# An adaLN block with linear attention and a GEGLU FFN: small stretches of the middle stage joined, loads around the second LayerNorm put in another order, and one bfloat16 run for each pair of the down projection

## The chip, the core and the metric

The kernel runs on one NeuronCore of a Trainium2 chip. A core has a matrix engine (TensorE, in profiles PE, with its weight loads as PEld), a vector engine (VectorE, DVE), a scalar engine (ScalarE, ACT), GpSimd (POOL) and SyncE (SP), which here issues nearly all DMAs. The engines run side by side and meet at semaphores. The metric is the device time of one execution in microseconds (us); lower is better.

## The reference

S = 2048 rows, D = 1024, 32 heads of 32, F = 3584; all inputs are bfloat16.

```python
def _A_ref(x, wqkv, wo):                       # linear attention
    qkv = (x @ wqkv).reshape(B, S, 3, H, Dh).transpose(2, 0, 3, 1, 4)
    q, k, v = qkv
    phi = lambda t: jnp.where(t > 0, t + 1, jnp.exp(t)) + 1e-06
    pq, pk = phi(q), phi(k)
    kv = jnp.einsum('bhsd,bhse->bhde', pk, v)
    z = jnp.einsum('bhsd->bhd', pk)
    num = jnp.einsum('bhqd,bhde->bhqe', pq, kv)
    den = jnp.einsum('bhqd,bhd->bhq', pq, z)[..., None] + 1e-06
    return (num / den).transpose(0, 2, 1, 3).reshape(B, S, D) @ wo

def _B_ref(x, w_gate, w_up, w_down):           # GEGLU FFN
    return _gelu(x @ w_gate) * (x @ w_up) @ w_down

mod = (_silu(c) @ w_mod).reshape(1, 6, 1, -1)
sa, ca, ga, sb, cb, gb = (mod[:, i] for i in range(6))
h = _layernorm(x) * (1 + ca) + sa
x = x + ga * _A_ref(h, A_wqkv, A_wo)
h = _layernorm(x) * (1 + cb) + sb
x = x + gb * _B_ref(h, B_w_gate, B_w_up, B_w_down)
```

## The kernel before

Every operation is recorded first, as an `Op` with its engine, the bytes it reads and writes, and what it must wait for (`Sched.op`). Each engine then runs its own list in order; `Sched.reorder` moves DVE, ACT and POOL operations between the first K tiles and the start of LN2 by planned costs, and everything behind it runs in the order in which it was recorded. SP runs its DMAs in order too, and a DMA takes one of eight lanes in turn and waits for the one that used the lane before (`Sched.dma`), so at most eight are under way.

Rows are tiled in 16 chunks of 128 and 4 groups (sg) of 4 chunks. The stages, with TensorE's time in the profiled execution:

- K and Q, to 127 us: LN1, modulation, K and Q products, phi. Values that depend on `c` are summed on DVE meanwhile.
- M, 127 to 191: instead of V, M = pk^T x is formed in 24 tiles of 16 matmuls (`m_tile`, L895, banks 0 to 3 of PSUM in turn), transposed by DMA (`m_t`, mtb) and multiplied with Wv (`kv_prod`, L913). Between tiles stand small stretches, set out by tile number in `HOOK` (L1302): rows of the modulation (`mod_rows`, L840, 32 columns of the array at a time), the denominators (`den`, L1240), and kv folded into Wo (`w2_pair`, L1201). `mod_pass` (modp) makes sb and cb, `gb_rows` (gbr) makes gb; `mod_pass` stores its row to HBM and loads it back by partition (sbT, cbT). `den` stores 1/den to HBM, and `rb_load` (L1260) brings it back, broadcast over partitions, in four DMAs of 256 KB for each half group; RB has two buffers, for even and odd groups.
- Wo, 191 to 241: `pq_scale` (L1273, DVE, four operations for a half group) multiplies pq by 1/den; `wo_mm` (L1283) multiplies chunk by chunk with the folded Wo into banks 2(c%4) and the next; x1 (L1291, DVE) adds the residual and gives the row sums. LN2 of the first 8 chunks runs beside it, one step each: mean on POOL, Square on ACT (`ln2_stats`, L674), xhat on ACT into one of four buffers xl (`ln2_rows`, L660), a DMA transpose (T2) into h2a or h2b, modulation on DVE (`mod2`, L724) or ACT. The Square writes the same buffer xl of its chunk, so that of chunk c+4 waits for T2 of chunk c. `SLOT` lists what stands behind each chunk.
- FFN, 241 to 600: `unit` (L1458) is one 256-wide strip of gate and up for half of the rows, by a Strassen-Winograd scheme of seven products of half size: P1 and P2 in bfloat16, the others of sums (`s_sum` of rows, L1413; `t_sum` of weights, L1433) in fp32r. Chunks 14 and 15 of Wo stand inside unit 0.
- Down, 600 to 777: the same scheme for pairs of chunks (`d_pair`, L1672 through `d_prod`, 14 matmuls a product, pairs 0 to 7): sums of y on DVE (`d_s`, L1648; sum k feeds P5, P6, P7, P3, P4 for k = 0 to 4, two buffers SB in turn), sums of weights (`d_t`, L1621), partial results added in PSUM (`d_add`, L1695), results scaled by gb and added to x (`evac`, L1576 and L1577). `y_in` loads y (ya0, ya1), `x_in` loads x (xq0 to xq3). In one pair the order is P1, P5, P6, P2, P7, P3, P4: P1 and P2 are bfloat16, so there are two bfloat16 runs.

Of the kernel before, what the change touches and what calls it, by code (L numbers as in the profile page):

```python
# [15 lines left out]
CPG = NCH // NSG  # L16
# [314 lines left out]
def bass_adaLN_cond__linear_attn_block__geglu_ffn__prompt_kernel(  # L331
# [18 lines left out]
    with ExitStack() as es:  # L350
# [554 lines left out]
        def m_t(g):  # L905
            i = g % 2
            tdma(Q, MTB[i][:, :, :], MB[g][:, :], r_mb(g), r_mtb(i), f"mT{g}")

        def kv_prod(g, bank):
            i = g % 2  # L910
            o = None
            for dc in range(NDC):
                o = sch.op(T, lambda e, dc=dc: e.matmul(PS(bank, 0, P), WV[:, g, dc, :], MTB[i][:, dc, :],  # L913
                                                        start=(dc == 0), stop=(dc == NDC - 1)),
                           rd=r_wv(g) + r_mtb(i), pwr=(pr(bank) if dc == 0 else ()), note=f"kv g{g} dc{dc}")
            pset_writer(bank, o)
            z = 64 * (g % 2)
            for h in range(2):
                a, gz = 64 * h, g // 2 * 2 + h
                sch.op(V, lambda e, a=a, gz=gz: e.tensor_tensor(KVT[z:z + 64, gz, 0:64], ps_all[a:a + 64, bank * 512 + a:bank * 512 + a + 64], BMASK[a:a + 64, a:a + 64], ALU.mult),  # L920
                       prd=pr(bank), rd=r_sm("bmask"), wr=r_kvt(gz, gz + 1), note=f"kvt{g}", overwrite_ok=True)
# [270 lines left out]
        def z32():  # L1192
            sch.op(V, lambda e: e.tensor_tensor(Z32[:], BM32[:], ZCOLS[:, :].unsqueeze(2).to_broadcast([P, NG, NH]), ALU.mult),
                   rd=r_sm("bm32") + r_sm("zcols"), wr=r_sm("z32"), note="z32")

        def w2_pair(i, b0=4):
            for hf in range(2):
# [6 lines left out]
            for r in range(2):  # L1204
                b, g = b0 + 2 * r, 2 * i + r
                w_, p_ = W2[:, g, :], ps_all[:, b * 512:(b + 2) * 512]
                eng = V if i > 1 and r else A
                sch.op(eng, lambda e, w_=w_, p_=p_, eng=eng: e.activation(w_, p_, ACTF.Copy) if eng == A else e.tensor_copy(w_, p_),
                       prd=pr(b) + pr(b + 1), wr=r_w(OFF_WK, "w2", g), note=f"w2cp{g}")
# [15 lines left out]
        def mod_pass():  # L1225
            assert mdone[0] >= 48 and not late
            mod_rows(((2, 4, 5, hl_src),))
            o_r = mod_store(4, 5, MROW[1], r_2k(OFF_ROW + 2048, "mrow1"), 1)
            for dst, nt, a0 in ((SBT, "sbT", 0), (CBT, "cbT", 2)):
                sch.dma(Q, lambda e, dst=dst, a0=a0: e.dma_start(dst[:, :], scr_row[1, a0:a0 + 2, :].rearrange("a (b p) -> p (a b)", p=P)),  # L1230
                        wr=r_sm(nt), deps=[o_r], note=nt)

# [33 lines left out]
        GH = [((0, 2), (2, 4)), ((4, 6), (6, 8))]  # L1266

        def pq_scale(sg, h, gs):
            i, t0 = sg % 2, h * HW
            for g0, g1 in gs:  # L1270
                ap = PQ[sg][:, g0:g1, t0:t0 + HW]
                rng = r_pq(sg, g0, g1, t0, t0 + HW)
                sch.op(V, lambda e, ap=ap, i=i, h=h, g0=g0, g1=g1: e.tensor_tensor(ap, ap, RB[i][:, h, g0:g1, :], ALU.mult),  # L1273
                       rd=rng + r_rb(i, h, g0, g1), wr=rng, deps=rb_ops[sg, h], note=f"pqs{sg}.{h}.{g0}")

        x1_ops, s_ops = {}, {}

        def wo_mm(c_, b0, gs):
# [9 lines left out]
            if gs[-1] == NG - 1:  # L1288
                for half in range(2):
# [11 lines left out]
        tiles = [(g, k) for g in range(4) for k in range(3)] + [(g, 0) for g in range(4, NG)] + [(g, k) for g in range(4, NG) for k in (1, 2)]  # L1301
        HOOK = {0: "ga", 6: "kv0", 10: "kv1", 11: "w0", 13: "kv2", 15: "modp kv3 z32", 16: "den0", 17: "w1 rb0.0 rb0.1", 18: "",  # L1302
                19: "kv4", 20: "den1 ps0.0", 21: "gbr", 22: "ps0.1", 23: "rb2.0"}
        st = {}

        def hook_run(f):
            if f[:2] == "kv":
                kv_prod(int(f[2:]), 4)
            elif f == "ga":
                ga_pass()  # L1310
            elif f == "gbr":
                assert mdone[0] == 64
                gb_rows()
            elif f == "modp":
                mod_pass()
            elif f == "z32":
                z32()
            elif f[:3] == "den":
                st[int(f[3:])] = den(int(f[3:]), 5)
                st[int(f[3:])]()  # L1320
            elif f[:2] == "ps":
                pq_scale(int(f[2]), int(f[4]), GH[0] + GH[1])
            elif f[:2] == "rb":
                rb_load(int(f[2]), (int(f[4]),))
            elif f[0] == "w":
                w2_pair(int(f[1:]))

        for n, (g, k) in enumerate(tiles):
# [19 lines left out]
            for f in HOOK.get(n, "").split():  # L1348
                hook_run(f)
        wo_mm(0, 0, [0, 1, 2, 3])  # L1350
        w2_pair(2)
# [16 lines left out]
        def wt_dma(u):  # L1368
            i, f0 = u % 2, u % NFP * 256
            for t, v_ in enumerate((wg_v, wu_v)):  # L1370
                sch.dma(Q, lambda e, t=t, v_=v_: e.dma_start(WT[i][:, t, :, :], v_[:, :, f0:f0 + 256]), wr=r_wt(i, t, t + 1), note=f"wt{t} u{u}")

# [224 lines left out]

        pq_scale(2, 0, GH[0] + GH[1])

# [55 lines left out]
        def d_prod(ca, b0, k, own=None, js=None):  # L1655
            b = b0 + {1: 0, 2: 0, 5: 3, 6: 2, 7: 2, 4: 2, 3: 1}[k] if own is None else own
            i = {1: None, 2: None, 5: 0, 6: 1, 7: 2, 3: 3, 4: 4}[k]
            o = None
            js = range(nj(ca)) if js is None else js
            for j in js:  # L1660
# [5 lines left out]
                else:  # L1666
# [3 lines left out]
                    if i == 4:  # L1670
                        dst = dst.rearrange("p (h c) -> p h c", h=2)
                o = sch.op(T, lambda e, l_=l_, r_=r_, j=j, dst=dst: e.matmul(dst, l_[:, 0, :], r_, start=(k in (1, 5) or own is not None) and j == js[0], stop=j == js[-1], skip_group_check=True),  # L1672
                           rd=rl + rr, pwr=(pr(b) if j == js[0] else ()), note=f"down P{k} c{ca} j{j}", overwrite_ok=True)
# [30 lines left out]
        def d_pair0(hook):  # L1704
            parts = parts_of(0)
            for k in (2, 6, 5, 0, 7, 3, 13, 11, 12, 4):
# [13 lines left out]
                hook(k)  # L1720

        def d_pair(i, hook):
            ca, b0 = 2 * i, i % 2 * 4
# [6 lines left out]

            for k in (1, 5, 6, 2, 7, 3, 4):
                if last and k == 3:
                    d_prod(ca, b0, 3, None, range(6, NDJ))
                    evac_part(*parts[1])
                    continue
                d_prod(ca, b0, k)
                if k == 1:
                    d_cp(b0 + 2, b0, "dpcp")
                elif k == 5:
                    d_ecp(b0 + 3)  # L1740
                    d_s(ca, 2)
                elif k == 6:
                    d_add(b0 + 1, b0 + 2)
                    d_s(ca, 3)
                    y_next(0)
                elif k == 2:
                    evac(*parts[0])
                elif k == 7:
                    d_add(b0 + 3, b0 + 2)
                    d_s(ca, 4)  # L1750
                    y_next(1)
                    evac(*parts[3])
                elif k == 3:
# [130 lines left out]
        def hooks(i):  # L1884
            def hook(k):
                more = i + 1 < 2 * CPG
                if i == 1:
                    if k == 1:
                        d_t(2, 5)
                        d_t(2, 6)  # L1890
                    if k in (6, 2, 7):
                        d_t(4, {6: 4, 2: 5, 7: 6}[k])
                    if k in (6, 7):
                        n = 1 if k == 6 else 2
                        evac(*parts_of(0)[n])
# [12 lines left out]
        for i in range(1, 2 * CPG):
            d_pair(i, hooks(i))
# [75 lines left out]
```

## Time and profile before

| what | value |
|---|---|
| runs | 783.5, 783.53 and 1619.89 us; median 783.53 |
| the profiled execution, first to last instruction (span) | 780.9 us; its own time is not listed beside it |
| granted TensorE clock | 1.000 |
| TensorE in the first 24 us | warm-up matmuls, transposes and waits for the first loads |
| HBM read and written | 92.55 and 23.35 MB, 148 GB/s over the span |

Busy time of engines in five stretches around the start of LN2 (us of busy time; DMA is the mean busy share of the 16 DMA engines):

| stretch | length | PE | DVE | ACT | DMA share | GB/s |
|---|---|---|---|---|---|---|
| 190 to 206 | 16 | 15.79 | 10.98 | 4.86 | 0.92 | 198 |
| 206 to 222 | 16 | 15.89 | 15.19 | 11.23 | 1.08 | 235 |
| 222 to 241 | 19 | 18.89 | 16.81 | 13.31 | 1.13 | 252 |
| 241 to 254 | 13 | 12.95 | 12.41 | 6.15 | 0.90 | 243 |
| 254 to 261 | 7 | 7.00 | 6.89 | 2.71 | 0.00 | 0 |

How to read the lines below. A timeline line has start, duration, engine (SPq is SyncE's queue of DMA issues), source line, operation, output <- inputs, shapes, how many alike in a row, and in brackets how long the engine had been idle and what ended that. Matmuls are pipelined, so their durations overlap; the distance between starts is what counts. Some matmul records are missing (13 instead of 14 of a product). A line of waits has who waited, for whom, us in total, times, longest.

### The profile page before, as it was taken

The numbers are of one execution on the slowest core, as the hardware profiler recorded it, in microseconds if no ns is written. First come the engines' busy times: TensorE is split into PE (matmuls) and PEld (weight loads), VectorE is DVE, ScalarE is ACT, GpSimd is POOL, SyncE is SP. The second block draws the span as 40 slices with busy tenths as digits, with TensorE's granted clock in tenths as the row PEclk, the third lists the DMA queues.
The fourth block names the chain that finished last, engine by engine and source line by source line (L and its number), as shares of the span: only waits on it lengthen the run. The fifth ranks groups of instructions, "written<-read, shape, count | busy, mean of one in ns | idle before, by whom it ended". The sixth has DMA issues, their size and how long they took to land.

```text
span 780.9 us, 10753 instructions
## 1 busy us (share of the span) xinstructions
PE 770.2 (99%) x3825; PEld 496.2 (64%) x3883; DVE 645.9 (83%) x964; ACT 374.6 (48%) x629; POOL 47.5 (6%) x126
## 2 busy tenths in 40 slices
PE   8999999999999999999999999999999999999998
PEld 4444445666445667667676767667676576677766
DVE  6699988897899878787989888888989888676767
ACT  2497743242466487878755555555555211111111
POOL 2031300000321011100000000000000000000000
PEclk9999999999999999999999999999999999999999
DMA  9879749939999358867353865535356334443331
GB/s 284 256 167 252 158 91 215 255 80 196 203 287 231 82 138 212 230 175 215 99 145 108 250 211 172 148 96 161 97 147 221 111 127 139 144 141 114 126 125 60
DMA packets 196940, 130.22 MB, mean 167 GB/s; under 512 B 69516, under 2 KB 182420, under 8 KB 195864
## 3 DMA queue, kind: packets, MB, share of 16 engines
q1 hardware_dynamic: 196872, 129.55, 62.4%
q8 instruction: 30, 0.49, 0.3%
q14 instruction: 22, 0.18, 0.1%
q10 hardware_dynamic: 16, 0.00, 0.0%
HBM read 92.55 MB, written 23.35 MB: 148 GB/s over the span
## 4 chain that ended last, share of the span: by engine, by line
PE 95%; SPq 2%; DMA 1%; DVE 1%; issue 1%; ACT 0%; DVEq 0%; ACTq 0%
PE ps_all L1458 45%; PE ps_all L1672 21%; PE ps_all L895 7%; PE ps_all L934 7%; PE ps_all L1283 7%; PE ps_all L880 5%; PE ps_all L1593 1%; SPq L598 1%; DMA wmq<-in_w_mod_dram 1%; SPq L603 1%; DMA h1T<-xh 0%; PE ps_all L913 0%; PE ps_all L1201 0%; PE ps_all L1240 0%; DVE h1T L724 0%
## 5 line engine op out<-in xcount | busy, mean ns | idle before, releaser
L1458 PE MATMUL ps_all<-ss,tp 128*128 128x512 f32 x896 | 214.3, 396 | 0.0
L1458 PEld LDWEIGHTS ps_all<-ss,tp 128*128 128x128 f32 x896 | 168.3, 188 | 37.8 <-DVE ss L1413 0.2
L1672 PE MATMUL ps_all<-dt,sb 128*128 128x512 f32 x424 | 102.5, 398 | 0.0
L1481 ACT ACTIVATE ge<-ps_all 128x512 f32<-128x512 f32 x112 | 64.1, 597 | 73.8 <-DVE ps_all L1469 62.1
L1458 PE MATMUL ps_all<-h2a,wt 128*128 128x512 bf16 x421 | 95.7, 379 | 1.8
L1672 PEld LDWEIGHTS ps_all<-dt,sb 128*128 128x128 f32 x424 | 79.6, 188 | 18.5 <-DVE sb L1648 0.3
L1476 DVE TENSOR_TENSOR ps_all<-ps_all,es 128x512 f32<-128x512 f32 x54 | 37.6, 699 | 49.4 <-ACT es L1466 49.0
L1488 DVE TENSOR_TENSOR ys<-ge,ps_all 128x512 bf16<-128x512 f32 x112 | 74.4, 684 | 3.8 <-PE ps_all L1672 0.5
L1458 PEld LDWEIGHTS ps_all<-h2a,wt 128*128 128x128 bf16 x448 | 38.0, 98 | 57.3 <-ACT ps_all L1463 16.9
L1433 DVE TENSOR_TENSOR tp<-wt 128x1024 fp32r<-128x1024 bf16 x56 | 68.1, 1217 | 1.8 <-DMA wt<-in_B_w_up_dram 1.8
L1433 DVE TENSOR_TENSOR tp<-wt,tp 128x1024 fp32r<-128x1024 bf16 x56 | 68.2, 1218 | 0.0
L934 PE MATMUL ps_all<-h1T,wq 128*128 128x512 bf16 x256 | 56.7, 379 | 0.0
L880 PE MATMUL ps_all<-wk,h1T 128*128 128x512 bf16 x239 | 55.3, 379 | 1.1 <-DMA wk<-in_A_wqkv_dram 0.5
L1283 PE MATMUL ps_all<-w,pq 128*128 128x512 bf16 x249 | 55.7, 379 | 0.5 <-issue 0.2
L1458 PE MATMUL ps_all<-ar,tp 128*128 128x512 f32 x224 | 55.5, 390 | 0.0
L869 ACT ACTIVATE eb<-ps_all 128x512 f32<-128x512 f32 x64 | 36.3, 594 | 37.6 <-PE ps_all L880 16.0
L1672 PE MATMUL ps_all<-wd,ya 128*128 128x512 bf16 x199 | 47.5, 380 | 0.7
L1458 PEld LDWEIGHTS ps_all<-ar,tp 128*128 128x128 f32 x224 | 42.1, 188 | 8.9
L1463 ACT ACTIVATE ps_all<-ps_all 128x512 f32<-128x512 f32 x56 | 32.6, 582 | 26.8 <-PE ps_all L1458 26.5
L934 PEld LDWEIGHTS ps_all<-h1T,wq 128*128 128x128 bf16 x256 | 25.0, 98 | 30.0
L1283 PEld LDWEIGHTS ps_all<-w,pq 128*128 128x128 bf16 x256 | 24.6, 98 | 30.3 <-issue 1.1
L1643 ACT ACTIVATE sb<-ya 128x896 fp32r<-128x896 bf16 (+1 forms) x16 | 14.5, 913 | 58.8 <-PE ps_all L1672 58.8
(141 smaller groups left out, 976.3 us busy)
## 6 DMA issues: line engine op xcount, KB each, us to landing
wt<-in_B_w_gate_dram SPq DMA_DIRECT2D x28, 512.0 KB, 4.0
wt<-in_B_w_up_dram SPq DMA_DIRECT2D x28, 512.0 KB, 5.2
scr_y<-ys SPq DMA_DIRECT2D x28, 512.0 KB, 3.2
ya<-scr_y SPq DMA_DIRECT2D x14, 896.0 KB, 4.9
rb<-scr_rd SPq DMA_DIRECT2D x32, 256.0 KB, 6.0
wd<-in_B_w_down_dram SPq DMA_DIRECT2D x7, 1024.0 KB, 7.6
wmst<-in_w_mod_dram SPq DMA_DIRECT2D x6, 1024.0 KB, 6.2
wmq<-in_w_mod_dram SPq DMA_DIRECT2D x8, 512.0 KB, 7.5
```

Source lines behind the costliest of these rows:

```text
L869: sch.op(A, lambda e: e.activation(EB[i][:, :], PS(bank), ACTF.Exp), prd=pr(bank), wr=rng, note=f"{note}.exp")
L880: o = sch.op(T, lambda e, dc=dc: e.matmul(PS(bank), H1[sg][:, ci, dc, :], W_[:, dc, jg * 512:(jg + 1) * 512], start=(dc == 0), stop=(dc == ...
L895: o = sch.op(T, lambda e, c_=c_: e.matmul(PS(bank, 0, n), PK[c_][:, g * P:(g + 1) * P], xrow(c_, o_, o_ + n), start=(c_ == 0), stop=(c_ == ...
L934: o = sch.op(T, lambda e, dc=dc: e.matmul(PS(b), WQ[:, dc, qc * P:(qc + 1) * P], H1[sg][:, :, dc, :], start=(dc == 0), stop=(dc == NDC - 1 ...
L1283: last[half] = sch.op(T, lambda e, g=g, half=half: e.matmul(PS(b0 + half), PQ[sg][:, g, ci * P:(ci + 1) * P], W2[:, g, half * 512:(half + ...
L1433: sch.op(V, lambda e: e.tensor_tensor(TP[k][:], in0, in1 if k in (0, 2) else in1[:], ALU.subtract), rd=r0 + r1, wr=r_tp(k), deps=[x1_ops[7 ...
L1458: o = sch.op(T, lambda e, l_=l_, r_=r_, dc=dc: e.matmul(PS(b), l_, r_, start=fresh and dc == 0, stop=dc == ND2 - 1, skip_group_check=True) ...
L1463: sch.op(A, lambda e: e.activation(PS(BB + t), PS(BA + t), ACTF.Copy), prd=pr(BA + t), pwr=pr(BB + t), note="pcp")
L1476: sch.op(V, lambda e: e.tensor_tensor(PS(BC + t), PS(BC + t), ES[t][:, :], ALU.add), prd=pr(BC + t), rd=r_2k(OFF_ES[t], f"es{t}"), pwr=pr( ...
L1481: sch.op(A, lambda e: e.activation(GE[i][:, :], PS(b), ACTF.Gelu_apprx_tanh), prd=pr(b), wr=r_2k(OFF_GE[i], f"ge{i}"), note="gelu")
L1488: sch.op(V, lambda e: e.tensor_tensor(YS[s_][:, 2 * h:2 * h + 2, t, :], q(GE[i][:, :]), q(PS(b + 1)), ALU.mult), rd=r_2k(OFF_GE[i], f"ge{i ...
L1672: o = sch.op(T, lambda e, l_=l_, r_=r_, j=j, dst=dst: e.matmul(dst, l_[:, 0, :], r_, start=(k in (1, 5) or own is not None) and j == js[0] ...
```

## The change

In M, `modp` moves from tile 15, `w1` from 17 and `gbr` from 21 to where the denominators are made (tiles 16 and 20), in other PSUM banks, so that three and two small stretches stand together. The loads of sbT and cbT leave `mod_pass` and stand behind tile 22. Of the rb loads, both halves of sg 1 come first and then both of sg 2; before, the first half of sg 2 was ahead. The x rows of chunks 7 to 9 and the weights of unit 0 are issued right behind them, ahead of the first T2; before, they stood behind the first and the third T2. The scale of the first half of sg 1 is pinned ahead of x1 of chunk 0; that of sg 2 is split, two operations behind x1 of chunk 2 and two behind x1 of chunk 4; x1 of chunks 0 to 2 are pinned in their order.

In the down stage P1 of the next pair is computed behind P2 of this one (`d_open`): order P5, P6, P7, P2, P1 of the next, P3, P4. P7 gets the bank of P5, started anew, and is copied out and added to both sums (`d_join`, one copy on ACT and one addition on DVE more for each of pairs 1 to 6). ya1 is loaded behind P2 and x rows at other points. Pairs 0 and 7 keep their order but for P1 of pair 7.

```diff
-            mod_rows(((0, 2, 5, lambda j, h: (HLG[:, j, h, :], r_hlg(j, h))),))
-            o_gb[0] = mod_store(2, 5, MRG, [(OFF_TMP + 4096, OFF_TMP + 5120, "mrg")], 2)
+            mod_rows(((0, 2, 6, lambda j, h: (HLG[:, j, h, :], r_hlg(j, h))),))
+            o_gb[0] = mod_store(2, 6, MRG, [(OFF_TMP + 4096, OFF_TMP + 5120, "mrg")], 2)
...
         def mod_pass():
-            mod_rows(((2, 4, 5, hl_src),))
-            o_r = mod_store(4, 5, MROW[1], r_2k(OFF_ROW + 2048, "mrow1"), 1)
+            mod_rows(((2, 4, 2, hl_src),))
+            o_sc[0] = mod_store(4, 2, MROW[1], r_2k(OFF_ROW + 2048, "mrow1"), 1)
+        def mod_load():
             for dst, nt, a0 in ((SBT, "sbT", 0), (CBT, "cbT", 2)):
...
-                       deps=[s_ops[0, 0, 1]] if c_ == 13 else [], note=f"x1 c{c_}")
+                       deps=[s_ops[0, 0, 1]] if c_ == 13 else o_pq if c_ == 0 else [x1_ops[c_ - 1]] if c_ < 3 else [], note=f"x1 c{c_}")
...
-        HOOK = {0: "ga", 6: "kv0", 10: "kv1", 11: "w0", 13: "kv2", 15: "modp kv3 z32", 16: "den0", 17: "w1 rb0.0 rb0.1", 18: "",
-                19: "kv4", 20: "den1 ps0.0", 21: "gbr", 22: "ps0.1", 23: "rb2.0"}
+        HOOK = {0: "ga", 6: "kv0", 10: "kv1", 11: "w0", 13: "kv2", 15: "kv3 z32", 16: "modp den0 w1", 17: "rb0.0 rb0.1", 18: "",
+                19: "kv4", 20: "den1 gbr ps0.0", 22: "sbl ps0.1"}
...
-                st[int(f[3:])] = den(int(f[3:]), 5)
+                st[int(f[3:])] = den(int(f[3:]), (3, 5)[int(f[3:])])
...
         rb_load(1)
-        rb_load(2, (1,))
+        rb_load(2)
+        x_dma(NXR, 10)
+        wt_dma(0)
         w2_pair(3)
         wo_mm(1, 2, [3, 4, 5])
         wo_mm(2, 4, list(range(6)))
+        o_pq = pq_scale(1, 0, GH[0] + GH[1])
         for c_ in range(3):
             wo_mm(c_, 2 * c_, [6, 7])
...
-        pq_scale(2, 0, GH[0] + GH[1])
+        after.update({(2, 0, 0): [x1_ops[2]], (2, 0, 2): [x1_ops[2]]})
+        pq_scale(2, 0, GH[0])
...
+        def d_join(b0):
+            d_ecp(b0 + 3)
+            d_add(b0 + 3, b0 + 1)
+            d_add(b0 + 2, b0 + 2)
+
+        def d_open(i):
+            b = i % 2 * 4
+            d_prod(2 * i, b, 1)
+            d_cp(b + 2, b, "dpcp")
...
-            for k in (1, 5, 6, 2, 7, 3, 4):
+            for k in ((5, 6, 2, 7, 3, 4) if last else (5, 6, 7, 2, 1, 3, 4)):
...
+                if k == 1:
+                    d_open(i + 1)
+                    hook(k)
+                    continue
                 d_prod(ca, b0, k)
...
+                elif k == 7:
+                    if last:
+                        d_add(b0 + 3, b0 + 2)
+                    else:
+                        d_join(b0)
+                    d_s(ca, 4)
+                    evac(*parts[3])
                 elif k == 2:
+                    y_next(1)
                     evac(*parts[0])
...
-        SLOT = {2: lambda: (pq_scale(1, 0, GH[0] + GH[1]), x_dma(NXR, 10)),
+        SLOT = {2: lambda: None,
                 3: lambda: pq_scale(1, 1, GH[0] + GH[1]),
-                4: lambda: (cb1(), wt_dma(0)),
+                4: lambda: (cb1(), after.update({(2, 0, 4): [x1_ops[4]], (2, 0, 6): [x1_ops[4]]}), pq_scale(2, 0, GH[1])),
                 5: lambda: (pq_scale(2, 1, GH[0] + GH[1]), rb_load(3, (0,))),
...
         d_pair0(hook0)
+        d_open(1)
+        d_t(2, 5)
+        d_t(2, 6)
```

More of the change, by code (lines that the diff above doesn't have):

```diff
@@ L919, in kv_prod @@
                 a, gz = 64 * h, g // 2 * 2 + h
-                sch.op(V, lambda e, a=a, gz=gz: e.tensor_tensor(KVT[z:z + 64, gz, 0:64], ps_all[a:a + 64, bank * 512 + a:bank * 512 + a + 64], BMASK[a:a + 64, a:a + 64], ALU.mult),
+                kvt_op[0] = sch.op(V, lambda e, a=a, gz=gz: e.tensor_tensor(KVT[z:z + 64, gz, 0:64], ps_all[a:a + 64, bank * 512 + a:bank * 512 + a + 64], BMASK[a:a + 64, a:a + 64], ALU.mult),
                        prd=pr(bank), rd=r_sm("bmask"), wr=r_kvt(gz, gz + 1), note=f"kvt{g}", overwrite_ok=True)
@@ L1266, in bass_adaLN_cond__linear_attn_block__geglu_ffn__prompt_kernel @@
         GH = [((0, 2), (2, 4)), ((4, 6), (6, 8))]
+        after = {}
         def pq_scale(sg, h, gs):
-            i, t0 = sg % 2, h * HW
+            i, t0, ops = sg % 2, h * HW, []
             for g0, g1 in gs:
@@ L1349, in bass_adaLN_cond__linear_attn_block__geglu_ffn__prompt_kernel, with wt_dma @@
                 hook_run(f)
+        def wt_dma(u):
+            i, f0 = u % 2, u % NFP * 256
+            for t, v_ in enumerate((wg_v, wu_v)):
+                sch.dma(Q, lambda e, t=t, v_=v_: e.dma_start(WT[i][:, t, :, :], v_[:, :, f0:f0 + 256]), wr=r_wt(i, t, t + 1), note=f"wt{t} u{u}")
         wo_mm(0, 0, [0, 1, 2, 3])
@@ L1655, in d_prod @@
         def d_prod(ca, b0, k, own=None, js=None):
-            b = b0 + {1: 0, 2: 0, 5: 3, 6: 2, 7: 2, 4: 2, 3: 1}[k] if own is None else own
+            b = b0 + {1: 0, 2: 0, 5: 3, 6: 2, 7: 3 if 0 < ca < 4 * CPG - 2 else 2, 4: 2, 3: 1}[k] if own is None else own
             i = {1: None, 2: None, 5: 0, 6: 1, 7: 2, 3: 3, 4: 4}[k]
@@ L1671, in d_prod @@
                         dst = dst.rearrange("p (h c) -> p h c", h=2)
-                o = sch.op(T, lambda e, l_=l_, r_=r_, j=j, dst=dst: e.matmul(dst, l_[:, 0, :], r_, start=(k in (1, 5) or own is not None) and j == js[0], stop=j == js[-1], skip_group_check=True),
+                o = sch.op(T, lambda e, l_=l_, r_=r_, j=j, dst=dst: e.matmul(dst, l_[:, 0, :], r_, start=(k in (1, 5) or k == 7 and 0 < ca < 4 * CPG - 2 or own is not None) and j == js[0], stop=j == js[-1], skip_group_check=True),
                            rd=rl + rr, pwr=(pr(b) if j == js[0] else ()), note=f"down P{k} c{ca} j{j}", overwrite_ok=True)
@@ L1904, in hook @@
                             t_gb(q)
+                if more and k in (1, 4):
+                    x_in(i + 1, 3 if k == 1 else 0)
             return hook
         d_pair0(hook0)
+        d_open(1)
+        d_t(2, 5)
+        d_t(2, 6)
         for i in range(1, 2 * CPG):
```

43 lines of the change are left out of this document (17 added, 26 removed).

## The prediction

> **What bounds the kernel now.** I read the page first, then TensorE's waits from 100 us on, then its timeline in the three places that the diff touches, then the DVE, ACT and SP timelines around the start of LN2.
>
> ```profile
> span 780.9 us, 10753 instructions
> ...
> PE 770.2 (99%) x3825; PEld 496.2 (64%) x3883; DVE 645.9 (83%) x964; ACT 374.6 (48%) x629; POOL 47.5 (6%) x126
> ...
> PE 95%; SPq 2%; DMA 1%; DVE 1%; issue 1%; ACT 0%; DVEq 0%; ACTq 0%
> ```
>
> ```profile
> PE ps_all L1283 <- issue: 0.2, 1, 0.2
> ```
>
> TensorE is busy for 99% of the span and carries 95% of the chain. After 100 us it waits once, for 0.2 us. So the change can win only what TensorE spends between matmuls, and can lose wherever it makes TensorE wait. The span of the profiled execution is 780.9; the median of the runs is 783.53, so 2.6 us lie around the span, and I leave them as they are.
>
> Timeline of TensorE in M (two tiles, three small stretches):
>
> ```profile
> 168.09 1.18 PE L895 MATMUL ps_all<-xrow,pk 128*128 128x342 bf16 x7
> 169.11 1.47 PE L895 MATMUL ps_all<-xall,pk 128*128 128x342 bf16 x9
> 170.51 1.06 PE L1240 MATMUL ps_all<-pq,z 128*32 128x256 bf16 x32
> ...
> 175.51 1.47 PE L895 MATMUL ps_all<-xall,pk 128*128 128x342 bf16 x9
> 176.81 1.18 PE L895 MATMUL ps_all<-xrow,pk 128*128 128x342 bf16 x7
> ```
>
> Nine matmuls ahead of another tile last 176.81 - 175.51 = 1.30 from start to start; ahead of a small 128*32 stretch they last 170.51 - 169.11 = 1.40. Entering a small stretch costs 0.10.
>
> Timeline of TensorE in one down pair:
>
> ```profile
> 677.02 3.19 PE L1672 MATMUL ps_all<-wd,ya 128*128 128x512 bf16 x13
> 679.86 6.75 PE L1672 MATMUL ps_all<-dt,sb 128*128 128x512 f32 x28
> 686.45 3.33 PE L1672 MATMUL ps_all<-dh,sb 128*128 128x512 f32 x14
> 689.62 3.20 PE L1672 MATMUL ps_all<-wd,ya 128*128 128x512 bf16 x13
> ...
> 699.06 3.19 PE L1672 MATMUL ps_all<-wd,ya 128*128 128x512 bf16 x13
> ```
>
> A pair is 699.06 - 677.02 = 22.04. Its 28 bf16 matmuls at 0.216 (13.83 us for 64 in the chain, L934) and 70 f32 ones at 0.2265 (L1672 dh: 3.17 for 14) are 21.91. The 0.13 left belong to two bf16 runs: 0.065 for one.
>
> The timelines of SP, DVE and ACT where LN2 starts, one fence each:
>
> ```profile
> 192.51 12.38 SPq L1260 DMA_DIRECT2D rb<-scr_rd  x16
> 209.87 1.23 SPq L703 DMA_TRANSPOSE h2a<-xl  x1
> ...
> 219.10 3.13 SPq L703 DMA_TRANSPOSE h2a<-xl  x1
> 222.33 1.92 SPq L1260 DMA_DIRECT2D rb<-scr_rd  x4
> ```
>
> ```profile
> 205.38 3.09 DVE L1273 TENSOR_TENSOR pq<-pq,rb 128x512 bf16<-128x512 bf16 x5
> ...
> 224.04 1.23 DVE L1433 TENSOR_TENSOR tp<-wt 128x1024 fp32r<-128x1024 bf16 x1 [1.80 <-DMA wt<-in_B_w_up_dram]
> ...
> 229.78 2.50 DVE L1273 TENSOR_TENSOR pq<-pq,rb 128x512 bf16<-128x512 bf16 x4
> ```
>
> ```profile
> 216.08 1.15 ACT L674 ACTIVATE xl<-xall,mv 128x1024 bf16<-128x1024 bf16 x1 [1.75 <-POOL mv L664]
> ```
>
> What to see: sixteen rb loads are issued in one go, the first LN2 transpose (T2 0) follows 5 us later, and the rb loads of sg 3 stand right behind the fourth transpose (T2 3). DVE scales pq as soon as rb is there, waits 1.80 for the weights, and is just in time for the scale at 229.78. On ACT, 216.08 is the fifth Square of LN2. The DMA engines are the second bound here: share 0.92 to 1.13 from 190 to 241 us in the table by stage. DVE is nearly as full: 16.81 of 19 us from 222 to 241, 12.41 of 13 from 241 to 254.
>
> **Part by part.**
>
> M. modp (tile 15) and w1 (tile 17) move to den0 (tile 16), gbr (21) to den1 (20). Five entries become two: 3 x 0.10 plus 0.01 each on the way out = -0.32. The matmuls are the same. New waits: bank 2 and 3 at tile 16 were copied out by ACT one and two tiles (2.3 us each) earlier; gbr needs the last hlg, which the new order puts behind kvt4. Bounded by 0 and by 0.4, I take 0 (DVE ends it near 182.9, gbr's second half starts at 182.95).
>
> One page doubts part of this. TensorEngine Tiling (Array Packing) of the Trainium skill, "Key Properties", says that changing the tiling mode drains TensorE; by it the switch from 128*32 to 64*64 inside the joined stretch would still pay 0.10, M would give 0.22, the rb loads below would issue 0.10 later and the sum would be 784.5. No row of this trace has the two modes side by side.
>
> sbT and cbT (0.37 and 0.57 us of issue) move on SP from behind modp to ahead of the last mtb transpose. SP idles there (189.0 to 191.15), and their reader is cb1T at 213.1: nothing.
>
> The rb loads. 16 loads of 256 KB land one each 1.17 us (SP's issue is spaced so after the first eight). M ends 0.3 earlier, so the first is issued at 192.15 and groups of four land near 199.4, 204.1, 208.8 and 213.4. Group two of sg 1 is now first: pqs1.0 runs at 199.4 to 201.9, x1 c0 to c2 end at 205.4 as before. Then pqs2.0, pinned behind x1 c2, must wait for the third load group: DVE, in order, idles 3.4 us to 208.8, with x1 c3, pqs1.1 and all else behind it. Walking on with the old durations (a scale 0.61, x1 1.15), x1 c6 ends at 221.0 instead of 218.8. TensorE does not feel that: chunk 6 needs pqs1.1 at 213.6 and has its first slice at 211.9.
>
> x rows and the first weights. They now stand ahead of T2 0, so wt lands near 219 and the 1.80 wait at 224.04 goes; DVE is 0.4 late after it. But T2 0 lands behind them. Before, the last rb landed at 215.1 (10.5 after issue) and T2 0, issued 5.3 us later, at 216.0 (6.1): transfers of this queue land in order. x took 2.0 (218.0 after 216.0), a wt 1.84 (5.4 after 218.43, 4.2 after 217.80), a transpose 0.9. So T2 0 lands at 213.4 + 2.0 + 3.7 + 0.9 = 220.0. It holds xl0, which the fifth Square (216.08 on ACT) overwrites: that goes to 220.1. Behind it on ACT stands xhat 3 (ended 218.46), now 222.5; T2 3 issues at 222.55, and rb3.0 behind it on SP goes from 222.33 to 223.8 (a transpose issue of 1.23; 3.13 if its ring is full again, then 225.7). It lands 1.5 later, at 231.2, and the scale that DVE began at 229.78 begins then: 1.4 late. From there to 251.9 DVE has one idle of 0.29, so the last S sum before P7 of unit 0 is 1.1 late and ends at 253.0. TensorE, 0.3 ahead from M, was due there at 251.7 and before started at 251.95 to 252.1. Net against before: **+1.0** (M's gain is spent in it). Ends: -0.32 if DVE catches up, +2.9 with the 3.13 issue.
>
> Down pairs. P2 of a pair and P1 of the next become one bf16 run: 14 runs become 8 (d_open(1), six, the last P2). 6 x 0.065 = **-0.39**; ends 0 and -0.39. Added for each of six pairs: one more descp on ACT (0.60; ACT sits idle 7 us there) and one more dpadd on DVE (0.70, pitch 0.61; DVE idles 1 to 2 us at four places of a pair). What is lost is cover: P5 followed P1 (3.0 us); now it follows P4 directly. Its S sum waits for P3's evacuation: 1.7 after P3's end (688.1 - 686.45), plus 1.04 for the first half, is 2.7 against 3.17 of P4. Fits by 0.4. P7 likewise follows P6; its sum is done 1.2 before. The y loads: ya0 is issued behind the third sum, near P6's end, and lands 4.5 to 6.0 later; P1 of the next pair starts 6.2 after. ya1 goes behind P2 and has 7.4 us for 4.8. In pair 1 DVE has the dt and dh sums too: it is busy from 628.67 to 647.06 with 0.18 idle, so with 0.61 more the first half for pair 2 is ready at 648.7, and TensorE is there at 626.4 + 22.0 = 648.4. **+0.3**; ends 0 and 1.0.
>
> Sum: 1.0 - 0.39 + 0.3 = +0.9 on the profiled span: 781.8, and 783.53 + 0.9 = **784.4**.
>
> **Rivals.**
>
> A, DVE catches up: T2 0 lands by 218 or the fifth Square does not hang on it. For: in the trace that Square also follows POOL's mean (215.42 + 0.58). Against: landings in order. Then -0.32 - 0.39: 782.8.
>
> B, slower, at the hand-over from pair to pair: ya1 later than DVE. DVE waited 1.15 and 1.34 us for ya1 at 667.25 and 689.49, covered by P1. If 1.34 stays, 1.34 - 0.4 = 0.9 in six pairs, 5.6 in all: 789.7. It starts to cost where ya1 lands over 7.4 us after its issue, and passes 2% at 10. Against it: ya1 is issued one product earlier against its reader than before, and landings here are 4.3 to 6.0.
>
> C, joining does nothing: the slower first matmuls after a bf16 run are only how ends are modelled, and the down gain is 0: 784.4 + 0.4 = 784.8, or 785.2 with gbr waiting 0.4 too.
>
> **How the numbers follow.** Forecast 0.48 (783.4 to 785.6), A 0.27, C 0.12, B 0.10, B beyond 2% 0.03. The range reaches from A, 782.7, to 786.1 (the forecast's upper part with C). About 2% is what a measurement of this kernel can tell from no change, 15.7 us; only B beyond its point gets there. Faster 0.01, same 0.96, slower 0.03.
>
> **What would show it.** M: tiles 17, 18 and 22 without the 0.10; TensorE out of M 0.3 earlier. DVE idle before a pq scale near 205 to 209, no wait for wt, ACT's fifth Square near 220, rb3.0's issue near 224, TensorE waiting for DVE (L1413's sums) near 252. Down: pair starts 21.97 apart, one wait near 648. I am wrong if TensorE leaves unit 0 no later than before, or if single pairs take over 22.3.

## The result and the profile after

The changed kernel takes 784.34 us (median of 12 runs, 783.32 to 785.9). The kernel before, run beside it, takes 783.09 (12 runs). The ratio is 1.0021, with a 95% interval of 1.0012 to 1.0029: slower by 0.9 to 2.3 us, far within 2%. One of the 12 runs before took 1619.89 us, twice as long as any other, and the ratio leaves it out. The profiled execution of the changed kernel has a span of 782.3 against 780.9.

The two spans can't be compared to a tenth. M begins 126.8 us into the profile after and 127.4 into the one before, and in the eleven other profiles of this study it begins anywhere from 126.9 to 128.2, whatever the kernel, so the difference lies ahead of M. So stages are compared from start to start of TensorE's matmuls (from its timeline), counted from the start of M. They repeat to a few hundredths, but for two: down, where a wait of up to 0.4 for a y load comes and goes (179.68 in e3 and 179.42 in e7, below), and Wo in kernels where TensorE has to wait for DVE at its end. e10, which is the changed kernel up to the down pairs, has 45.40 there, 0.46 less than the table; so the sum below is good to about half a microsecond:

| us | before | after | difference |
|---|---|---|---|
| M, to its last tile | 61.71 | 61.39 | -0.32 |
| to the last fold (w2) in Wo | 7.31 | 7.31 | 0 |
| Wo from there to unit 0 | 45.03 | 45.86 | +0.83 |
| unit 0 | 19.70 | 21.39 | +1.69 |
| the other units | 337.41 | 337.35 | -0.06 |
| down, to the last matmul | 179.38 | 179.13 | -0.25 |
| sum | 650.54 | 652.42 | +1.88 |

To set a time of the changed kernel's profile beside one of the profile before, add 0.58 to it (127.40 - 126.82).

The first line of the changed kernel's page, and below it TensorE's waits from 100 us on (total, times, longest):

```profile
span 782.3 us, 10828 instructions
```

```profile
PE ps_all L1475 <- DVE xall L1303: 1.2, 2, 0.7
PE ps_all L1475 <- DVE ss L1430: 0.5, 2, 0.3
```

Before there was one wait of 0.2. Now there are four, all in unit 0 (L1475), all for DVE: twice for an x1 that still has to empty the bank, twice for an S sum. The first of them (0.67) stands ahead of unit 0's first matmul and so counts in the table's row for Wo. Start to start they cost more than the 1.7 listed, because a busy PE is drawn to a modelled end.

TensorE's timeline at the two joined stretches in M, DVE's at the second of them, and TensorE's in one down pair:

```profile
167.87 1.47 PE L895 MATMUL ps_all<-xall,pk 128*128 128x342 bf16 x9
169.27 0.62 PE L840 MATMUL ps_all<-hl,ones 128*32 128x512 bf16 x8
169.71 1.05 PE L1248 MATMUL ps_all<-pq,z 128*32 128x256 bf16 x32
170.69 0.63 PE L1205 MATMUL ps_all<-wo,kvt 64*64 64x512 bf16 x8
...
172.28 1.47 PE L895 MATMUL ps_all<-xall,pk 128*128 128x342 bf16 x9
173.59 1.18 PE L895 MATMUL ps_all<-xrow,pk 128*128 128x342 bf16 x7
...
181.09 1.06 PE L1248 MATMUL ps_all<-pq,z 128*32 128x256 bf16 x32
181.98 0.62 PE L840 MATMUL ps_all<-hlg,ones 128*32 128x256 bf16 x8
182.53 1.19 PE L895 MATMUL ps_all<-xrow,pk 128*128 128x342 bf16 x7
```

```profile
181.56 0.69 DVE L804 TENSOR_TENSOR hlg<-gacc,hlg 128x512 bf16<-128x512 f32 x1 [0.77 <-ACT hlg L803]
```

```profile
681.65 6.22 PE L1690 MATMUL ps_all<-wd,ya 128*128 128x512 bf16 x28
...
703.63 6.22 PE L1690 MATMUL ps_all<-wd,ya 128*128 128x512 bf16 x28
```

The timeline of den1 in the kernel before, where the next tile follows it:

```profile
182.00 1.06 PE L1240 MATMUL ps_all<-pq,z 128*32 128x256 bf16 x32
182.99 1.19 PE L895 MATMUL ps_all<-xrow,pk 128*128 128x342 bf16 x7
```

Both joins take away what they were meant to. Nine matmuls ahead of the one stretch still last 1.40 (169.27 - 167.87), but the next tile's nine last 1.31 (173.59 - 172.28). The way out of a stretch counts too: den1's matmuls last 0.89 up to gbr (181.98 - 181.09), which uses the array in the same way, and before they lasted 0.99 up to the next tile. modp's last 0.44 up to den0 (169.71 - 169.27) instead of 0.55 up to a 128*128 product (167.64 - 167.09 in the profile before). Against that gbr now waits: its last two matmuls need the rest of `hlg`, which DVE ends at 182.25, and start at 182.31, 0.22 behind the two before them. So gbr takes 0.55 (182.53 - 181.98) instead of 0.34 (185.76 - 185.42 before). The list of waits does not have this one.

In the down pairs, one bf16 run of 28 matmuls a pair is left where two of 14 were, and a pair is 703.63 - 681.65 = 21.98 instead of 22.04.

The timelines of SP, ACT and DVE where LN2 starts:

```profile
191.58 12.97 SPq L1268 DMA_DIRECT2D rb<-scr_rd  x16
205.53 0.40 SPq L592 DMA_DIRECT2D xall<-in_A_x_dram  x1
...
207.92 3.94 SPq L1367 DMA_DIRECT2D wt<-in_B_w_up_dram  x1
211.96 12.53 SPq L703 DMA_TRANSPOSE h2a<-xl  x4
224.58 1.92 SPq L1268 DMA_DIRECT2D rb<-scr_rd  x4
```

```profile
220.81 1.15 ACT L674 ACTIVATE xl<-xall,mv 128x1024 bf16<-128x1024 bf16 x1 [5.36 <-DMA h2a<-xl]
```

```profile
209.24 1.29 DVE L1283 TENSOR_TENSOR pq<-pq,rb 128x512 bf16<-128x512 bf16 x2 [3.89 <-DMA rb<-scr_rd]
...
225.01 1.22 DVE L1450 TENSOR_TENSOR tp<-wt 128x1024 fp32r<-128x1024 bf16 x1
...
231.89 2.50 DVE L1283 TENSOR_TENSOR pq<-pq,rb 128x512 bf16<-128x512 bf16 x4 [1.21 <-DMA rb<-scr_rd]
```

DVE idles 3.89 ahead of pqs2.0. It no longer waits for the weights (225.01). The fifth Square waits 5.36 for T2 0, rb3.0 is issued at 224.58, and DVE idles again, 1.21, ahead of the scale of sg 3. On the clock of the profile before, that scale starts at 232.47 instead of 229.78: DVE is 2.7 late, and unit 0 pays for it.

### The profile page after: what moved, and what is told of

Same layout as the page of the kernel before. It is cut to its first block, busy times and chain, and to the rows that moved or that the text cites. A ratio compares the mean times of both kernels' runs of the same rounds, so it can differ in the third digit from the quotient of the medians.

```text
span 782.3 us, 10828 instructions
## 1 busy us (share of the span) xinstructions
PE 774.6 (99%) x3883; PEld 497.5 (64%) x3883; DVE 647.4 (83%) x970; ACT 376.6 (48%) x635; POOL 47.6 (6%) x126
## 4 chain that ended last, share of the span: by engine, by line
PE 88%; SPq 5%; DMA 4%; DVE 2%; issue 1%; POOL 0%; ACT 0%; DVEq 0%; POOLq 0%
PE ps_all L1475 44%; PE ps_all L1690 21%; PE ps_all L895 7%; PE ps_all L936 7%; PE ps_all L880 6%; DMA rb<-scr_rd 3%; SPq L703 2%; PE ps_all L1610 1%; DMA wmq<-in_w_mod_dram 1%; SPq L598 1%; SPq L603 1%; DVE ss L1430 1%; DVE pq L1283 1%; SPq L1367 1%; PE ps_all L1295 0%
## 5 line engine op out<-in xcount | busy, mean ns | idle before, releaser
L1475 PE MATMUL ps_all<-ss,tp 128*128 128x512 f32 x896 | 214.5, 396 | 1.0 <-DVE xall L1303 0.5
L1475 PEld LDWEIGHTS ps_all<-ss,tp 128*128 128x128 f32 x896 | 168.1, 188 | 39.7 <-DVE ss L1430 1.4
L1475 PE MATMUL ps_all<-h2a,wt 128*128 128x512 bf16 x448 | 101.5, 380 | 0.7 <-DVE xall L1303 0.7
L1475 PEld LDWEIGHTS ps_all<-h2a,wt 128*128 128x128 bf16 x448 | 37.9, 98 | 58.2 <-ACT ps_all L1480 16.9
L1475 PE MATMUL ps_all<-ar,tp 128*128 128x512 f32 x224 | 55.5, 390 | 0.0
L1716 ACT ACTIVATE de<-ps_all 128x512 f32<-128x512 f32 x14 | 8.4, 597 | 90.2 <-PE ps_all L1690 90.2
L1475 PEld LDWEIGHTS ps_all<-ar,tp 128*128 128x128 f32 x224 | 42.0, 188 | 8.9
```

The lines of the kernel that those rows point to most:

```text
L1475: o = sch.op(T, lambda e, l_=l_, r_=r_, dc=dc: e.matmul(PS(b), l_, r_, start=fresh and dc == 0, stop=dc == ND2 - 1, skip_group_check=True) ...
```

## The experiments

The theory: the whole loss is made by the LN2 part, which makes DVE late in two ways, by its idle ahead of pqs2.0 (the new rb order) and by the scale of sg 3 waiting at the end of the chain T2 0, fifth Square, xhat 3, T2 3, rb3.0 (x rows and weights ahead of T2 0). The rivals: the loss is in the down pairs; or the joins do nothing; or only one half of the LN2 part counts. Ratios are to the kernel before, run beside each.

**The parts alone.** Three kernels take one part of the diff each onto the kernel before, a fourth takes the two joins without the LN2 part. e1: the LN2 part.

```
-                19: "kv4", 20: "den1 ps0.0", 21: "gbr", 22: "ps0.1", 23: "rb2.0"}
+                19: "kv4", 20: "den1 ps0.0", 21: "gbr", 22: "ps0.1"}
...
-        rb_load(2, (1,))
+        rb_load(2)
+        x_dma(NXR, 10)
+        wt_dma(0)
...
+        o_pq = pq_scale(1, 0, GH[0] + GH[1])
...
```

> The kernel before with only the LN2 part of the change: the new order of the rb loads, the pins on the pq scales, and x rows and the first weights ahead of T2 0. M and the down pairs are as before. Theory 1 (the whole loss is made here: DVE runs late from pqs2.0 and again from the scale of sg 3, and TensorE waits for it at the start of unit 0): unit 0's end comes 1.3 to 1.9 later than before, the time is 1.3 to 1.9 us above before, and everything behind unit 0 is shifted by the same amount. Rival 2 (the loss is made in the down pairs, at their hand-over): 0 here. Rival 3 (DVE catches up): within 0.3 of before.

Measured: 784.88, ratio 1.0026 (1.0018 to 1.0035). Wo takes 45.58, unit 0 21.39; from the start of M to the end of unit 0 it is 135.99 us, against 133.75 before and 135.95 in the changed kernel. So the whole loss, +2.24, is here, above the 1.3 to 1.9 that were expected. Set beside the changed kernel, M's 0.32 shows only as 0.04 behind unit 0, since TensorE waits for DVE there. But e10, the same kernel as the changed one up to the down pairs, takes 135.51 for this, so how much of the 0.32 is left there stays open.

e2: the down pairs' part alone (`d_open`, `d_join`, the order 5, 6, 7, 2, 1, 3, 4 and the hooks, as in the diff).

> The kernel before with only the down pairs' part: P2 of a pair and P1 of the next in one bfloat16 run. Theory 1: pair starts 21.97 apart instead of 22.04, one wait of 0.2 to 0.3 in pair 1: 0.1 to 0.2 us below before. Rival 2 (the hand-over costs): above before by 0.9 or more, with TensorE waiting at P5 of every pair. Rival C (joining does nothing): pair starts 22.04 apart, 0.2 to 0.4 above before.

Measured: 782.85, ratio 0.9999 (0.999 to 1.0008). Down takes 179.02 instead of 179.38, -0.36, without a wait at P5. A gain of 0.36 is 0.05%, too little for the times. The stage shows it.

e3: the joined stretches in M alone; e4: those and the down pairs' part. Both keep rb2.0 at tile 23:

```
-        HOOK = {0: "ga", 6: "kv0", 10: "kv1", 11: "w0", 13: "kv2", 15: "modp kv3 z32", 16: "den0", 17: "w1 rb0.0 rb0.1", 18: "",
-                19: "kv4", 20: "den1 ps0.0", 21: "gbr", 22: "ps0.1", 23: "rb2.0"}
+        HOOK = {0: "ga", 6: "kv0", 10: "kv1", 11: "w0", 13: "kv2", 15: "kv3 z32", 16: "modp den0 w1", 17: "rb0.0 rb0.1", 18: "",
+                19: "kv4", 20: "den1 gbr ps0.0", 22: "sbl ps0.1", 23: "rb2.0"}
...
```

> The kernel before with only the joined small stretches in M (and the row loads split off behind them). Theory 1: tiles 17, 18 and 22 lose their 0.10, TensorE leaves M 0.32 earlier and nothing behind gives it back: 0.3 us below before. By the rule that a switch between two modes drains TensorE as well: 0.22 below. Rival C: 0, with gbr's wait up to 0.4 above.

> The joined stretches in M and the joined runs of the down pairs, with the LN2 part as before. Theory 1: both gains without the loss: 0.4 to 0.6 us below before and 1.6 to 2.0 below the changed kernel. Rival 2: no better than the changed kernel. Rival C: no different from before.

Measured: 782.81 and 783.01, ratios 0.9998 (0.9989 to 1.0007) and 1.0002 (0.9993 to 1.0011). In both, M takes its 0.32 less (61.39, 61.38), and Wo gives it back: 45.45 instead of 45.03. I had not expected that. TensorE's waits of e4:

```profile
PE ps_all L1291 <- DVE pq L1281: 0.2, 1, 0.2
```

and DVE around it:

```profile
205.35 3.69 DVE L1281 TENSOR_TENSOR pq<-pq,rb 128x512 bf16<-128x512 bf16 x6
```

With the old order, DVE's second run of pq scales reaches the groups that TensorE reads next just as TensorE comes to them. TensorE is there 0.3 earlier and waits: one start comes 0.62 after the one before it, instead of 0.22. The rb loads that feed those scales don't come earlier: in e3 they are issued 0.34 earlier behind M's start, and the first of them lands 68.7 us behind it as before. In sum: the joins in M are worth 0.32 in M and nothing behind Wo, as long as DVE keeps that order.

**Which half of the LN2 part.** e5 puts x rows and weights back, e6 the old order of rb loads and scales, e7 the weights only. All three keep the rest of the change. The edit of e5:

```
-        x_dma(NXR, 10)
-        wt_dma(0)
...
-        SLOT = {2: lambda: None,
+        SLOT = {2: lambda: x_dma(NXR, 10),
...
-                4: lambda: (cb1(), after.update({(2, 0, 4): [x1_ops[4]], (2, 0, 6): [x1_ops[4]]}), pq_scale(2, 0, GH[1])),
+                4: lambda: (cb1(), after.update({(2, 0, 4): [x1_ops[4]], (2, 0, 6): [x1_ops[4]]}), pq_scale(2, 0, GH[1]), wt_dma(0)),
```

> The changed kernel with x rows and the first weights put back behind T2 0 and behind the mod2 wait (as before); the new order of the rb loads and the pins stay. Theory 1 (two causes that add up: DVE idles about 4 us ahead of pqs2.0, and T2 0, the fifth Square, rb3.0 and the scale of sg 3 are late behind x and the weights): T2 0 lands near 216, the fifth Square runs by 217, rb3.0 lands near 229.8, DVE does not wait for it and reaches it about 0.9 later than in the kernel before; unit 0's start to unit 1's start 20.1 to 20.6 (before 19.7, changed kernel 21.4), the time 0.8 to 1.3 below the changed kernel. Rival 2 (the rb order alone): 21.4, no different from the changed kernel. Rival 3 (x and weights alone): 19.7, 1.7 below.

> The changed kernel with the order of the rb loads and the pq scales of before (no pins), x rows and the first weights still ahead of T2 0. Theory 1: DVE does not idle near 205 to 209, but T2 0 lands near 220, the fifth Square follows it, rb3.0 lands near 231.8 and the scale of sg 3 starts there, 1.9 later than in the kernel before; unit 0's start to unit 1's start 21.0 to 21.4, within 0.4 of the changed kernel. Rival 2 (the rb order alone): 19.7, 1.7 below the changed kernel.

> The changed kernel with only the weights put back; x rows stay ahead of T2 0. Theory 1: T2 0 lands at 214.6 + 2.0 + 0.9 = 217.5, the fifth Square near 217.6, rb3.0 near 230; DVE reaches the scale of sg 3 by its own lateness (0.9 over before), so much the same as with both put back: unit 0's start to unit 1's start 20.1 to 20.8. Rival 2 (the rb order alone): 21.4. Rival 3 (only DVE's wait for x rows and weights counts): 19.7.

Measured: e5 783.28, ratio 1.0002 (0.9993 to 1.001), unit 0 20.36. e6 784.91, ratio 1.0025 (1.0016 to 1.0034), unit 0 21.37. e7 783.23, ratio 1.0002 (0.9993 to 1.0011), unit 0 20.34. Wo is 45.03 in e5 and e7 (the new rb order takes away e4's wait for a pq scale) and 45.98 in e6, which has that wait again. In e5 TensorE waited 0.3 for an mtb transpose besides, which none of the other kernels so far did. ACT in e6, the fifth Square (in e7 it starts at 217.31, after a wait of 1.70):

```profile
222.32 1.15 ACT L674 ACTIVATE xl<-xall,mv 128x1024 bf16<-128x1024 bf16 x1 [7.57 <-DMA h2a<-xl]
```

DVE in e6, the scale of sg 3:

```profile
233.33 2.50 DVE L1283 TENSOR_TENSOR pq<-pq,rb 128x512 bf16<-128x512 bf16 x4 [1.06 <-DMA rb<-scr_rd]
```

Both halves cost, and they do not add up as I had said: x rows and weights ahead of T2 0 cost unit 0 1.67 with the old rb order (e6), the new rb order without them 0.66 (e5), both together 1.69. It is a maximum: whatever DVE lost near 205 it would have lost again later. In e6 DVE has no idle near 205 and waits instead 3.58 ahead of the first modulation of h2a and 1.06 for rb3.0. The weights are the expensive transfer, not the x rows (unit 0 is 20.34 in e7, 20.36 in e5): with x alone ahead of it T2 0 frees its buffer by 217.3 and DVE reaches the scale of sg 3 (230.25) after rb3.0 has landed (229.56).

**The last links of that chain.** e11 issues rb3.0 ahead of T2 3 and leaves x and weights where the change puts them.

```
-                4: lambda: (cb1(), after.update({(2, 0, 4): [x1_ops[4]], (2, 0, 6): [x1_ops[4]]}), pq_scale(2, 0, GH[1])),
-                5: lambda: (pq_scale(2, 1, GH[0] + GH[1]), rb_load(3, (0,))),
+                4: lambda: (cb1(), after.update({(2, 0, 4): [x1_ops[4]], (2, 0, 6): [x1_ops[4]]}), pq_scale(2, 0, GH[1]), rb_load(3, (0,))),
+                5: lambda: pq_scale(2, 1, GH[0] + GH[1]),
```

> The changed kernel with one more move on SP: rb3.0 (four loads) is issued ahead of T2 3 and no longer behind it; x rows and the first weights stay ahead of T2 0. Theory 1 (x and the weights cost only through T2 0, the fifth Square, xhat3, T2 3 and rb3.0 queued behind it): rb3.0 is issued near 221.0 and lands near 228.5, DVE does not wait ahead of the scale of sg 3 and is late only by its idle ahead of pqs2.0 (0.9 over before); unit 0's start to unit 1's start 20.1 to 20.6 instead of 21.4, 0.8 to 1.2 below the changed kernel. Rival (the two transfers themselves take the room, or T2 3 behind the loads is late next): 21.0 or more.

Measured: 785.01, ratio 1.0026 (1.0015 to 1.0037), unit 0 21.37: no gain there. Wo is 45.35, no shorter than the 45.40 of e10, which lacks this edit. DVE:

```profile
229.03 2.14 DVE L724 TENSOR_SCALAR h2a<-h2a,cb1T,sbT 128x256 bf16<-128x256 bf16 x8 [1.33 <-DMA h2a<-xl]
```

rb3.0 landed at 228.1, as expected, and DVE no longer waits for it. Now it waits 1.33 for T2 3, which was late behind xhat 3 all along, and the scale of sg 3 starts at 232.2. So the rival holds in its second form: rb3.0 was the last of several late things. With e7, where T2 0 lands earlier and unit 0 takes 1.05 less, the root is T2 0's landing.

**Rows early.** e8 is e4 with the loads of sbT and cbT moved from tile 22 to tile 18, to see whether they hold the rb loads back.

```
-        HOOK = {0: "ga", 6: "kv0", 10: "kv1", 11: "w0", 13: "kv2", 15: "kv3 z32", 16: "modp den0 w1", 17: "rb0.0 rb0.1", 18: "",
-                19: "kv4", 20: "den1 gbr ps0.0", 22: "sbl ps0.1", 23: "rb2.0"}
+        HOOK = {0: "ga", 6: "kv0", 10: "kv1", 11: "w0", 13: "kv2", 15: "kv3 z32", 16: "modp den0 w1", 17: "rb0.0 rb0.1", 18: "sbl",
+                19: "kv4", 20: "den1 gbr ps0.0", 22: "ps0.1", 23: "rb2.0"}
```

> Joined stretches in M and joined runs in the down pairs, LN2 part as before, and the loads of sbT and cbT moved from tile 22 up to tile 18, ahead of sg 0's last stretch. Theory 1 (in the M-and-down kernel TensorE waits 0.41 at 206.7 to 207.3 for a pq scale, because the small packets of sbT and cbT, some 2060 more of them between 180 and 216, stand ahead of the rb loads and push their first landing back by the 0.3 that M wins): the first rb of the second set lands 68.4 behind M's start (68.7 there), the wait shrinks to 0.1 or less, the time is 0.3 to 0.4 below the M-and-down kernel, 0.5 to 0.7 below before. Rival 2 (the rb loads are bound by their own 1.17 us each, wherever the rows stand): the wait stays at 0.4 and the time is that of the M-and-down kernel.

Measured: 783.83, ratio 1.0015 (1.0006 to 1.0024), a miss. SP:

```profile
181.91 6.25 SPq L703 DMA_TRANSPOSE mtb<-mb  x1
```

Behind eight rb loads and the two row loads, the issue of one mtb transpose took 6.25 us, and TensorE waited 1.4, once, for mtb. The wait for the pq scale is gone, but only because TensorE came later. Why the rb loads of e3 and e4 land no earlier than before stays open: this run spoilt what it was to measure.

**The hand-over of the pairs.** e10 issues ya1 one product later.

```
                     d_open(i + 1)
+                    y_next(1)
                     hook(k)
...
                 elif k == 2:
-                    y_next(1)
                     evac(*parts[0])
```

> The changed kernel with one load moved: the second half of the next pair's y (ya1) is issued behind P1 of the next pair and no longer behind P2, some 3.0 us later, in six pairs. It prices the hand-over's cover. Theory 1 (the cover is what the forecast's rival B says: ya1 has 7.4 us for 4.3 to 6.0): 4.4 us are left for 4.8, so TensorE waits 0 to 1.6 a pair, most likely 0.4, pairs 22.0 to 23.6 apart, 0 to 9 us in all, likely 2.4 above the changed kernel. Rival (ya1's landing does not set the sums, the evacuation of P3 does): pairs stay 21.97 apart, the time is that of the changed kernel.

Measured: 791.67, ratio 1.0114 (1.01 to 1.0128), down 7.9 longer than in the changed kernel. The size lies in the range, the place does not: pair 1 to 2 takes 29.77, the others 21.97 to 22.19. TensorE's waits, and SP in pair 1:

```profile
PE ps_all L1690 <- DVE sb L1666: 4.7, 1, 4.7
```

```profile
648.40 0.37 SPq L1588 DMA_DIRECT2D ya<-scr_y  x1
```

In pair 1, ya1 now stands on SP behind an xq load (issued at 647.96) that waits until the result evacuated from its buffer is stored, at 647.90: ya1 is issued at 648.40 instead of 642.99 and lands at 653.45. In the next pair the move delays the issue by about 1.4 and hides entirely. What the wait cost beyond 4.7 is told at the end.

**A version that keeps the gains.** e9 is e5, and gives DVE something to do in the gap: pqs1.1, whose rb lands near 204, ahead of x1 c3, and pqs2.0 behind it.

```
-        after.update({(2, 0, 0): [x1_ops[2]], (2, 0, 2): [x1_ops[2]]})
-        pq_scale(2, 0, GH[0])
+        pq_scale(1, 1, GH[0] + GH[1])
...
-                3: lambda: pq_scale(1, 1, GH[0] + GH[1]),
+                3: lambda: (after.update({(2, 0, 0): [x1_ops[3]], (2, 0, 2): [x1_ops[3]]}), pq_scale(2, 0, GH[0])),
```

> The changed kernel with two repairs of the LN2 part: x rows and the first weights back behind T2 0 and T2 2 (as before), and in DVE's order pqs1.1, whose rb lands near 204, ahead of x1 c3 and pqs2.0 behind x1 c3, in the place where DVE idled 3.9 us. Theory 1 (nothing else in the change costs anything, and the new rb order gives TensorE pqs1 early enough to keep M's 0.32): no wait in Wo (45.03 from its last fold to unit 0), 19.7 from unit 0's start to unit 1's start, 0.3 from M and 0.25 to 0.36 from the down pairs kept: 0.5 to 0.7 below before, 1.8 to 2.3 below the changed kernel. Rival (M's gain is always spent against DVE or the rb loads): 0.2 to 0.4 below before, with a wait of 0.3 or more in Wo or in unit 0.

Measured: 782.45 (before 782.63), ratio 0.9997 (0.9988 to 1.0006). From the start of M to the last matmul it is 649.76 us: 0.78 less than before, 2.66 less than the changed kernel. M 61.38, Wo 45.03, unit 0 19.66, down 179.05; the list of TensorE's waits is empty behind 100 us. DVE:

```profile
205.16 2.49 DVE L1283 TENSOR_TENSOR pq<-pq,rb 128x512 bf16<-128x512 bf16 x4
...
208.93 1.29 DVE L1283 TENSOR_TENSOR pq<-pq,rb 128x512 bf16<-128x512 bf16 x2
```

The idle of 3.89 is filled. Against the changed kernel the gain is clear from both its ratio and the stages; against the kernel before, the times can't tell 0.1%, and only the stages say that it is faster.

## Why the prediction was right, and where it was not

The sign and the mechanism of the loss were right, and the size within a microsecond. 784.4 stands beside 784.34, but that is luck: the kernel before ran at 783.09 in this comparison instead of 783.53, and the difference was +1.6 by the ratio and +1.88 by the stages, about twice the +0.9 of the forecast.

- M, -0.32: measured -0.32, because two wrong terms cancel. The way out of a stretch, priced at 0.01, is worth 0.10 to 0.11 where the same use of the array follows (den1 0.89 instead of 0.99, modp 0.44 instead of 0.55), so two exits saved 0.21 more than the forecast had. gbr's wait, taken as 0, cost 0.22, so gbr took 0.55 instead of 0.34. DVE did end `hlg` where the prediction had it (182.83 on the clock of before, forecast 182.9), but gbr's last matmuls could have started 0.22 earlier than they did. The ten kernels with the join all show this (M 61.38 or 61.39, against 61.71 in the three others). The sentence from "TensorEngine Tiling (Array Packing)" of the Trainium skill, "Key Properties", that a change of mode drains TensorE, gave 0.22 in the prediction. The trace agrees with the sentence: den0's matmuls last 0.98 up to the 64*64 product (170.69 - 169.71), as long as the 0.99 ahead of a full tile, where den1's last 0.89 in one mode. The 0.22 missed the 0.32 because it left out the two exits and the wait.
- M's gain spent: TensorE does wait for DVE in unit 0, but whether all of it is spent stays open (0.04 of it is left by e1 and the changed kernel, more by e10). That it would be spent with the old LN2 part as well (e3, e4) the prediction did not see: its rival A counted it as kept.
- sbT and cbT moved, nothing: TensorE has no wait behind it in the changed kernel.
- The rb order: DVE's idle 3.89 (forecast 3.4), x1 c6 ends at 221.83 on the clock of before (221.0). The prediction said that TensorE does not feel it in Wo: right (45.03 in e5 and e7). But by itself it costs unit 0 0.66, hidden in the changed kernel by the larger delay.
- **The term that was mis-sized: +1.0 at unit 0, measured +2.2** (0.83 + 1.69 - 0.32). The step that failed is the first of its chain: "groups of four land near 199.4, 204.1, 208.8 and 213.4", at 1.17 for a load. That 1.17 is the spacing of SP's issues. In the trace before, the ninth load is issued at 196.32, behind the first landing at 196.09, and the thirteenth at 200.88, behind the fifth landing at 200.86: each issue waits for the landing eight loads earlier, as the lanes ask, so the issues show the pace of the first eight alone. All 16 landings run from 196.09 to 215.11, which is 1.27 for each of 15 steps, and the last eight are 1.32 apart; the trace after has 1.29, with one step of 2.12. The prediction itself had the last landing before at 215.1, and 15 steps of 1.17 from 196.09 would end at 213.6. So the last rb landed at 215.2, not 213.4 (all on the clock of before). Everything behind it followed the working, 1.2 to 1.4 later: fifth Square 221.4 (forecast 220.1), rb3.0 issued 225.2 (223.8), scale of sg 3 232.5 (231.2), last S sum 254.2 (253.0). It had TensorE wait for S sums alone; the two longer waits, 0.67 and 0.55 ahead of and in unit 0, are for x1, which DVE reaches late as well.
- Down, -0.39: pairs are 21.97 to 21.98 apart instead of 22.04, as forecast, so rival C falls. The +0.3 at pair 1 to 2 was 0.05 (pair starts 637.66 and 659.68): the sum that was to be late, at 648.90 to 650.98, just kept up. One other wait of 0.13 for y makes -0.25 in all; e2, without that one, has -0.36.
- Rival A (DVE catches up) falls: in e1 and in the changed kernel DVE was never on time again before unit 1. Rival B did not come. e10 shows why its working was too simple: ya1's cover is ample in most pairs, and short in pair 1, where an xq load ahead of it on the queue decides.

## What to carry to other kernels

Price a queue of transfers by its landings, not by the spacing of its issues. A transfer moved up is paid by what it is moved past, and by all that hangs on that, here by a buffer that came free 5 us later; where an engine idles in its order, first look for an operation whose data is already there. A gain on the bounding engine is only a gain if the next wait behind it moves as well; follow it to the end of the next two stages before you count it.

## What the runs showed of the hardware

TensorE's clock after a wait of 4.7 us, in e10. A row of the table by stretch, with the granted clock ahead of the DMA share:

```profile
655.00:661.00 6.00, 6.00 (x15) 4.67 (x15) 4.94 (x6) 0.00 (x0) 0.00 (x0) 0.52 0.09 27
```

In steps of 1 us, the granted clock is 1.00 up to 653, 0.96 from 653 to 654, 0.50 from 654 to 660, 0.62 from 660 to 661 and 1.00 from then on. So it fell about 3.9 us into the wait (650.00 to 654.69) and came back about 6.1 us behind its end. In that time 14 matmuls start 0.40 to 0.59 apart, most of them 0.427, instead of 0.227: 2.9 us on top of the wait. With the 4.85 by which the wait stretches one start to start, that is the whole 7.8 by which this pair is longer than 21.97. "TensorE: Matmul & The Clock Gate" of the Trainium skill, "What's actually happening", says that the clock falls to half after an idle window of about 3.4 us. This agrees: the waits of 0.7 in the changed kernel and 1.4 in e8 left the clock at 1.00. So the wait of 4.7 had a second price, which those two had not; where between 1.4 and 3.9 us it begins, no run here shows.

What a change in the use of the array costs: going in from full width 0.09 to 0.10 (nine matmuls last 1.40 instead of 1.30 or 1.31), going from 128*32 back to full width 0.10 (den1, 0.99 instead of 0.89), and from 128*32 to 64*64 about as much (den0, 0.98 instead of 0.89).

The issue of a DMA can block SP for long: T2 0's for 6.2 us and a wt's for 3.94 in the changed kernel, an mtb transpose's for 6.25 in e8, each with six or seven transfers issued before it and not landed. What stands behind it on SP is then late although its data is ready. What the issue itself waits for, no run here shows.
